# One written-out order of all engines exchanged for another in a one-core attention and MLP kernel

## The chip, the cores and the metric

The kernel runs on one core of one Trainium2 chip. The metric is the device time of one execution in microseconds (us); the figure of a kernel is the median of several executions. A core has five engines that take their instructions in order, each from its own queue: TensorE (PE; its weight loads are shown as PEld), VectorE (DVE), ScalarE (ACT), GpSimd (POOL) and SyncE (SP), which here only issues DMAs. Engines wait for one another, and for DMAs, by semaphores.

## What is computed

Windowed attention with four sink positions, over 4 batches, 8 heads, 768 positions and head size 64, and then an MLP over the 3072 tokens of width 512:

```
scores = q @ k.T / 8, kept where key < 4 or 0 <= query - key < 128
a      = softmax(scores);   x = (a @ v), heads side by side: 3072 x 512
h      = x @ w_in           (512 x 2048)
out    = (h * sigmoid(1.702 h)) @ w_out      (2048 x 512)
```

Inputs and output are float32 in memory; the kernel works in float16 and adds up in float32.

## The kernel before

The 3072 tokens are 24 blocks of 128 (block b is the part b mod 6 of batch b div 6). `BLOCKS` has the four that open a batch first (0, 6, 12, 18), then the others. A block needs its own keys and those of the block ahead of it (the window), and the four sink keys of its batch.

The work is a list of about 970 operations, each a closure that issues a few instructions on one engine. Their names, with the block or group number behind:

- `k`, `q`, `v`: loads of a block, with a cast to float16, issued by GpSimd (L310 for blocks 0, 6, 12, 18, 1 and 2, in long runs; L318 for the others; L271 for v). `wi`, `wo`: four pieces each of the two weights (L324, L331), also by GpSimd. All these share one DMA queue.
- `zv`: zeroing of `vsb` (L228), allowed on VectorE or GpSimd. `vsb`: its filling per batch (L344).
- `tk`, `tq`: transposes of k and q on TensorE (L383, L412) for the first eight blocks, with the copies `ck`, `cq` out of PSUM on VectorE or ScalarE (L241, L245). From block 5 on `tqk`, a DMA transpose issued by SP (L429), does this for one or two blocks.
- `msk`: the mask of blocks that open a batch (L464); `sc`: scores (L478, L483); `snk`: scores of the sinks (L507).
- `pk`, `mx`, `sb`, `ssb`, `ms`: masking, row maxima and subtraction on VectorE (L535 to L596); `nb` and `bx` instead for blocks that open a batch; `ex`: exponentials on ScalarE (L606).
- `ta`, `ca`: transposes of the weights on TensorE and their copies (L650), for the first six blocks; `tat`: the same as a DMA transpose by SP (L681) for the others. `sp`, `so`: GpSimd selects what belongs to the block ahead and to the own one (L637).
- `av`: values (L705 to L712); `nm`: their division (L722, L723); `tx`, `cx` or `txd`: the transpose to xT on TensorE (L740) or by DMA (L753).
- `h`: first layer (L786), `g`: its gate, on ScalarE (L816) or, with `th`, on ScalarE and VectorE (L800, L807) for groups 0 to 2; `o`: second layer (L836); `ev`: copy out; `st`: store (L856). Layers run in groups: {0}, {6}, {12, 18}, then two blocks each: group 3 is {1, 2}, group 4 {3, 4}, group 5 {5, 7}, and so on to group 12, {22, 23}.

PSUM tiles are rings: three of tag `mm` (all transposes and both layers), two of `sc`, one of `av`.

The order of everything is written out by hand, as the string `ORDER` (L56 on): a sequence of operation numbers, with a letter behind the number where an operation may go to several engines (d VectorE, a ScalarE, p GpSimd, s SP). `Plan.emit` (L125) calls the closures in this sequence. The costs, DMA classes and keys given to `plan.add` are kept in `Op` and read by nothing when the kernel is built:

```
for word in order.split():
    choice = letter.get(word[-1])
    op = self.ops[int(word[:-1] if choice else word)]
    assert all(d.seq in seen for d in op.deps), op.name
    seen.add(op.seq)
    op.emit(choice) if len(op.eng) > 1 else op.emit()
```

The first operations of the queues that matter here, decoded from the string, in the kernel before:

```
POOL  k0 q0 q6 q18 v0 k6 k12 wi1 k2 q12 k1 k18 vsb3 wi0 v6 wi2 q1 wi3 v12 wo0 wo1 v18 q2 wo2 wo3 q4 k4 k3 q3 k5 q7 q5
PE    msk0 tk0 tq0 tq6 sc0 tq18 tk6 tk12 ta0_0 ta0_1 msk6 av0_1 sc6 tk2 av0_0 tq12 tk1 tx0 tk18 h0_1 ...
      ... o6_3 sc2 tq4 snk2 ta1_1 tk4 o0_3 tx18 snk4 tq3 tk3 ta1_0 h2_7
SP    ... tat5 tqk9 tat7 st1_ st2_ tqk11 tat8 txd7 tat9 tqk13
```

Of the kernel before, what the change touches and what calls it, by code (L numbers as in the profile page):

```python
# [52 lines left out]


ORDER = """
3a 9 0s 7 14 94 4a 6 8d 5a 15 98 10 12 11 1a 13 18 2s 100 24 96 16 107 17 20 102 95d 88 103a 104 99d 29 105a 127 21  # L56
106 108 128a 26 173 109 23 112 174a 110 101p 97d 111 125 113 148 126d 86 114 115 149d 19 129 116a 117 130 90 118a 121
27 131 122 225 92 132 119 150 226a 120 22 194 151a 133 135 123 87 134 171 124d 136 152 89 613 137 172d 25 195d 138 614
153 175 139a 30 615 140 142 154 141a 143 610 155 158 144 91 616 611 145 612 146 617 156 93 147d 196 157 618 631 159
197d 160 628 36 632 161 176 35 162d 629 633 163 177 630 164a 637 181 178 32 167 619 638 182 168 183 179 622 639 180  # L60
165 634 166 33 620 623 635 38 621 198 636 199 640 204 42 200 227 201 641 228a 205 39 184 642 202 185a 188 206 186 624
189 187a 203 209 28 190 169 207 643 208 191 31 210 170d 229 644a 282 40 232 230 645 215 283a 280 231 625 216a 43 235
281a 233 192 217 626a 285 258 193d 256 34 627 259a 211 234 667 257a 41 236 212a 655 286 37 668 237 649 304 656 669 213
240 260 657 214 650 646 266 218 239 651 652 647 44 263 658 648 653 45 238 261 654 661 241 659 46 262 670 660 662 267
242 671 243a 264 221 663 244 664 265 245 672 268 665 222 246 284 666 247a 219 269 248 287 673 270 220 249 676 674a 288
271 48 252 290 677 49 253 675 223 323 291 47 250 224a 678 251 292 254 679 255a 289 272 293 688 680a 294 305 681 273
306 311 690 689 295 308 51 684 307 50 312 274 691 696 685 309 52 682 275 697 313 686 683 310 325 704 314 687 326 315
324 698 327 330 694 296 328 316 276 695 331 699 297 277 361 705 329 55 344 692 332 53 345 343 333 693 300 54 334 346
278 700 301 317 349 298 701 347 318 279a 335 299 706 702a 350 57 302 707 703 348 303a 58 351 321 708a 720 56 352 322
353 709 722 399 721 382 710 383 354 362 336 711 319 365 723 712 368 337 718 320 713 60 363 724 719 364 369 59 338 725  # L70
716 366 61 726 370 717 367 714 339 381 371 715 340 372 384 727 355 341 732 387 342 385 356 728 388 733 62 373 386 729
64 390 389 419 734 63 391 730d 359 744 360 392 752 745 374 400 731 357 403 735 375 753 358 742 406 736a 66 740 737 743
67 746 741 65 401 738 747 402 404 750 739 407 376 751 748 405 409 393 377 754 749 408 378 394 760 410 379 420 380 69
761 426 70 423 421 755 411 422 68 427 439 762 440 457 756 424 428 763 429 425 757 764a 430 766 765 758d 412 776 431
767 774 413 759 395 495 775 438 396 73 777 778 444 71 441 768 779 445 72 397 769 772 442 398 788 773 446 416 443 770
417 432 780 447 771 448 789 433 414 75 782 415 74 790 781 418 783 76 434 449 791 435 458 792a 459 464 784 793 461 800
460 465 806 514 801 462 796 807 466 477 798 797 467 478 450 463 436 799 785 437 468 451 794 786d 497 79 787 476 498
804 482 795 77 469 479 452 78 802 483 805 480 816 803 484 810 485 453 808 481 470 454 486 496 455 811 499 471 456 502
516 817 500 81 809 812 487 503 82 818 501 80 504 813 505 517 506 819 814d 474 815 820d 832 475 821 488 824 833 507 472
489 834 473 552 825 515 84 835 535 518 828 83 521 836 829 536 85 522 490 837 822 519 826 523 823 508 491 844 827 520  # L80
509 492 524 534 525 493 830 537 494 540 838 538 831 845 526 541 839 539 590 573 542 846 574 543 553 544 840 559 556
847 527 841 848a 545 862 528 842a 849 510 863 864 843 511 856 865 554 850 555 857 546 560 512 851 858 513 547 557 854
859 561 529 855 852 558 530 860 853 562 563 866 531 872 532 572 861 533 873 575 578 548 564 867 576 549 874 579 868
577 875 581 580 869 582 876d 591 565 877 870d 550 594 871 888 566 551 583 882 597 889 592 884 593 595 569 883 878 570
885 596 886 879 598 880 887 584 599 567 881 600 890 568 601 585 900 571 894 901 891 602 588 902 589 892 895 893 910
603 903 911 914 904a 604 586 905 915 920 587 906 921 912 907 605 913 918 606 916 919 607 917 908 608 896 609 909 922
897 928 898a 923 899 929 924 930 940 931 941 944 932a 925 933 945 948 926a 936 927 949 938 937 942 939 934 943 946 935
956 947 950 957 951 958 952 962 953 963 954a 959 964 955 960a 965 961 966a 967
"""


# [64 lines left out]
def kernel(  # L156
# [207 lines left out]
    for pos, b in enumerate(BLOCKS):  # L364
# [9 lines left out]
        if b in OCT:  # L374
            parts = []
            before = used_slot.pop(SLOT[b], [])
            for w in (1, 0):
                tp = ps("mm", (P, 8, 4, 16), FP32, f"t{'qk'[w]}{b}")

                def t_qk(w=w, buf=buf, n=n, tp=tp):  # L380
                    for t in range(8):
                        for l in range(2):
                            nc.tensor.matmul(  # L383
                                tp()[64 * l : 64 * l + 64, t], buf()[:, n, w, t],
                                ident.rearrange("p (j l u) -> p l j u", l=2, u=16)[:, l], start=True, stop=True,
                            )
# [15 lines left out]
            o_qkt[b] = parts  # L402
        elif b in TQ:
            tp = ps("mm", (P, 8, P), FP16, f"tq{b}")
            parts = []
            before = used_slot.pop(SLOT[b], [])
            for w in (1, 0):

                def t_qk(w=w, buf=buf, n=n, tp=tp):
                    src = buf()[:, n, w].rearrange("p h d -> p (h d)")  # L410
                    for c in range(4):
                        nc.tensor.transpose(tp()[:, 4 * w + c], src[:, bass.ts(c, P)], ident)  # L412
# [12 lines left out]
            o_qkt[b] = parts  # L425
        elif n == 0:

            def t_qk(buf=buf, unit=unit, s=SLOT[b]):
                nc.sync.dma_start_transpose(  # L429
                    qkT[:, s : s + len(unit)].rearrange("p r c t -> p (r c) t"),  # L430
                    buf()[:, 0 : len(unit)].rearrange("p n w h d -> p (n w h d)"),
                )
# [26 lines left out]
        if r == 0:  # L459

            def mask(sc=sc, own=own):
# [437 lines left out]
```

## Time and profile before

| | |
|---|---|
| median of 3 runs | 235.01 us (234.93 to 235.21) |
| profiled execution | 236.26 us, span of its instructions 234.6 us |
| TensorE busy | 220.5 us |
| VectorE busy | 153.1 us |
| ScalarE busy | 145.9 us |
| GpSimd busy | 111.5 us |
| DMA | 32.07 MB |

The span runs from the first instruction to the last of one profiled execution; that execution's own time includes what lies around the span. Busy time is the union of an engine's instructions; a matmul's end is modelled. An idle stretch is put down to the event that came last before it ended. Line numbers are those of the kernel file; the copies out of PSUM all stand on the lines of the helper `copy` (L241, L245).

### The profile page before, as it was taken

Reading aid. Unit: us, or ns where it says so; the run is one execution under the profiler, and the core shown is the slowest. Engines: PE = TensorE matmul, PEld = TensorE weight load, DVE = VectorE, ACT = ScalarE, POOL = GpSimd, SP = SyncE. Lnnn points to the kernel's source line nnn. Section 1 sums busy time; section 2 is a strip of 40 time slices with the busy share of each in tenths; the row PEclk is TensorE's granted clock in tenths of the full one; section 3 lists DMA queues with packets and bytes.
Section 4 is the critical chain, followed back from the end, with each engine's and each line's share of the span. In section 5 each row is a group of like instructions: output and inputs, shape, how many; then the busy total and the mean of one; then the engine's idle time right before and its main releaser. Section 6 shows DMA issues by size and latency. Waiting matters only on the chain.

```text
span 234.6 us, 5452 instructions
## 1 busy us (share of the span) xinstructions
PE 220.5 (94%) x2202; PEld 151.6 (65%) x2202; DVE 153.1 (65%) x384; ACT 145.9 (62%) x226; POOL 111.5 (48%) x129
## 2 busy tenths in 40 slices
PE   0899999999999998898999999999999999999994
PEld 0669865776575685476487577586496595775763
DVE  4668889999789959838846498969755982120000
ACT  2556866975586884464385576887678477541632
POOL 8964545966367829449178082656240330300000
PEclk9999999999999999999999999999999999999999
DMA  5999999999999999999999999999951445121202
GB/s 82 177 197 199 199 197 171 186 160 70 171 210 140 130 202 145 113 232 120 135 258 126 189 134 127 102 267 100 137 140 21 109 110 95 48 39 50 90 2 89
DMA packets 120904, 32.07 MB, mean 137 GB/s; under 512 B 112016, under 2 KB 117936, under 8 KB 120880
## 3 DMA queue, kind: packets, MB, share of 16 engines
q0 software_dynamic: 69888, 13.64, 72.7%
q1 hardware_dynamic: 50512, 17.96, 40.3%
q8 instruction: 17, 0.28, 0.5%
q10 hardware_dynamic: 480, 0.13, 0.3%
q14 instruction: 7, 0.06, 0.1%
HBM read 27.46 MB, written 6.29 MB: 144 GB/s over the span
## 4 chain that ended last, share of the span: by engine, by line
PE 70%; DVE 18%; DMA 6%; POOL 3%; issue 1%; ACT 0%; POOLq 0%
PE o L836 28%; PE hT L786 28%; DVE mx L545 4%; DMA qkn<-in_q_dram 4%; PE sc L483 4%; DVE sc L535 3%; DVE mx L548 3%; DVE e L582 3%; DMA xT<-xn 2%; PE av L705 2%; PE av L710 2%; POOL qkn L310 2%; DVE gT L807 2%; DVE xn L723 2%; PE av L712 2%; DVE e L596 1%
## 5 line engine op out<-in xcount | busy, mean ns | idle before, releaser
L786 PE MATMUL hT<-xT,w_in 128*128 128x256 f16 (+1 forms) x832 | 94.1, 266 | 1.0 <-DMA xT<-xn 1.0
L836 PE MATMUL o<-w_out,gT 128*128 128x512 f16 (+2 forms) x400 | 91.5, 371 | 0.1
L786 PEld LDWEIGHTS <-w_in 128*128 128x128 f16 x832 | 74.2, 98 | 13.2 <-issue 2.7
L816 ACT ACTIVATE gT<-hT 128x512 f16<-128x512 f32 x80 | 46.2, 597 | 31.1 <-PE hT L786 30.9
L836 PEld LDWEIGHTS <-gT 128*128 128x128 f16 x400 | 36.3, 98 | 33.4 <-issue 1.1
L637 POOL TENSOR_SCALAR_AFFINE_SELECT atp<-at 128x1024 f16<-128x1024 f16 (+1 forms) x22 | 22.4, 1018 | 74.0 <-DMA at<-a 67.4
L545 DVE TENSOR_REDUCE mx<-sc 128x4 f32<-128x512 f32 x48 | 32.5, 682 | 0.6 <-PE sc L478 0.6
L535 DVE COPY_PREDICATED sc<-later,sc 128x512 f32<-128x512 uint16 x40 | 26.5, 690 | 8.9 <-PE sc L483 8.7
L582 DVE TENSOR_TENSOR e<-sc,mx 128x512 f32<-128x512 f32 x40 | 26.4, 682 | 0.0
L722 DVE RECIPROCAL rcp<-av 128x4 f32<-128x4 f32 x48 | 8.5, 177 | 27.2 <-PE av L712 25.1
L606 ACT ACTIVATE a<-e 128x1056 f16<-128x1056 f32 (+2 forms) x24 | 22.4, 935 | 4.1 <-issue 2.3
L271 POOL DMA_DIRECT2D v<-in_v_dram x24 | 21.5, 896 | 3.8 <-DMA w_out<-in_moe_w_out_dram 1.7
L637 POOL TENSOR_SCALAR_AFFINE_SELECT at<-at 128x1024 f16<-128x1024 f16 (+1 forms) x22 | 22.1, 1008 | 1.4
L606 ACT ACT_TABLE_LOAD x13 | 16.7, 1283 | 9.7 <-issue 5.8
L723 DVE TENSOR_TENSOR xn<-av,rcp 128x256 f16<-128x256 f32 x48 | 20.4, 424 | 1.7
L816 ACT ACT_TABLE_LOAD x14 | 18.0, 1283 | 3.5 <-PE hT L786 3.3
L710 PE MATMUL av<-v,at 128*128 128x65 f16 x192 | 17.6, 196 | 0.9 <-POOL at L637 0.9
L318 POOL DMA_DIRECT2D qkn<-in_q_dram x18 | 16.1, 894 | 3.8 <-DMA w_out<-in_moe_w_out_dram 2.6
L318 POOL DMA_DIRECT2D qkn<-in_k_dram x18 | 16.1, 892 | 2.6 <-DMA w_out<-in_moe_w_out_dram 1.5
L710 PEld LDWEIGHTS <-at 128*128 128x128 f16 x192 | 14.4, 99 | 4.4 <-POOL at L637 1.2
L245 ACT COPY osb<-o 128x512 f32<-128x512 f32 (+2 forms) x14 | 7.7, 555 | 13.3 <-PE o L836 9.6
L712 PE MATMUL av<-v,atp 128*128 128x65 f16 x160 | 15.1, 194 | 0.0
(57 smaller groups left out, 199.8 us busy)
## 6 DMA issues: line engine op xcount, KB each, us to landing
out_dram<-osb SPq DMA_DIRECT2D x23, 256.0 KB, 3.1
qkn<-in_k_dram POOLq DMA_DIRECT2D x24, 128.0 KB, 5.9
qkn<-in_q_dram POOLq DMA_DIRECT2D x24, 128.0 KB, 5.9
v<-in_v_dram POOLq DMA_DIRECT2D x24, 128.0 KB, 6.4
w_in<-in_moe_w_in_dram POOLq DMA_DIRECT2D x4, 512.0 KB, 10.2
w_out<-in_moe_w_out_dram POOLq DMA_DIRECT2D x4, 512.0 KB, 13.4
at<-a SPq DMA_TRANSPOSE x18, 3.3
qkT<-qkn SPq DMA_TRANSPOSE x10, 7.7
```

The source lines that it names most:

```text
L271: f"v{b}", POOL, 0.88, lambda b=b, view=view: nc.gpsimd.dma_start(v65[:, b, :, 0:D], view),
L318: lambda buf=buf, n=n, w=w, view=view: nc.gpsimd.dma_start(buf()[:, n, "qk".index(w)], view),
L535: nc.vector.copy_predicated(out=t()[:, :, :, own].rearrange("p l j s -> p (l j) s"), mask=later.unsqueeze(1).to_broadcast((P, 4, P)), data ...
L545: nc.vector.tensor_reduce(out=part, in_=t()[:, :, :, own], axis=AX.X, op=ALU.max)
L582: nc.vector.tensor_tensor(out=e32()[:, 512 * hf : 512 * hf + 512].rearrange("p (l j s) -> p l j s", l=2, j=2), in0=t()[:, :, :, own], in1= ...
L606: nc.scalar.activation(out=a16()[:, lo:hi], in_=e32()[:, lo:hi], func=AF.Exp, scale=scale)
L637: nc.gpsimd.affine_select(out=dst, in_=at()[:, lo : lo + num], pattern=[[0, num], [1 if own else -1, P]], compare_op=ALU.is_ge if own else ...
L710: nc.tensor.matmul(av()[:, i], at()[:, c], v65[:, b, h], start=(r == 0), stop=(r == 0))
L723: nc.vector.tensor_tensor(out=xn()[:, xi, 4 * hf : 4 * hf + 4].rearrange("p (j l) d -> p l j d", l=2), in0=av()[:, :, 0:D].rearrange("p (l ...
L786: nc.tensor.matmul(ht()[:, n].rearrange("p (n t) -> p n t", n=NT), w_in16[:, c, bass.ts(f, P)], t0()[:, i0 : i0 + NT, c], start=(c == 0), ...
L816: lambda fs=fs, gt=gt, ht=ht: nc.scalar.activation(out=gt()[:, fs[0] : fs[-1] + 1], in_=ht(), func=AF.Gelu_apprx_sigmoid),
L836: nc.tensor.matmul(po()[:, 0:width], gt()[:, F, bass.ts(t, P)], w_out16[:, F, c0 : c0 + width], start=(F == 0), stop=(F == NF - 1),)
```

## The change

The string `ORDER` is replaced as a whole; the operations are the same ones. Three planner costs are changed as well: they enter no instruction.

```diff
 ORDER = """
-3a 9 0s 7 14 94 4a 6 8d 5a 15 98 10 12 11 1a 13 18 2s 100 24 96 16 107 17 20 102 95d 88 103a 104 99d 29 105a 127 21
...
+1a 9 4s 10 11 8p 100 12 2a 7 6 13 0a 94 5a 98 3a 15 96 14 23 107 17 21 101d 26 104 95d 105a 20 102 99d 29 103a 171 97d
...
-                    f"t{'qk'[w]}{b}", PE, 0.45 if early else 0.376, t_qk, deps=[ld["qk"[w], b], o_ident],
+                    f"t{'qk'[w]}{b}", PE, 0.4 if early else 0.376, t_qk, deps=[ld["qk"[w], b], o_ident],
...
-                    f"t{'qk'[w]}{b}", PE, 0.44 if early else 0.226, t_qk, deps=[ld["qk"[w], b], o_ident],
+                    f"t{'qk'[w]}{b}", PE, 0.25 if early else 0.226, t_qk, deps=[ld["qk"[w], b], o_ident],
...
-                f"msk{b}", PE, 0.88 if early else 0.45, mask, deps=[o_bias0, o_identb], take=sc, key=K0 - 34
+                f"msk{b}", PE, 0.6 if early else 0.45, mask, deps=[o_bias0, o_identb], take=sc, key=K0 - 34
```

Decoded, the same queues in the changed kernel:

```
POOL  zv q0 k0 k18 k6 q12 k1 k12 k2 q6 v0 v6 q1 q18 wi1 wi3 wi2 wi0 wo0 v12 wo1 v18 q2 wo2 wo3 k3 q4 k4 q3 v1 v3 q5 k5
PE    msk0 tq0 tk0 tk18 sc0 tk6 tq12 tk1 tk12 tk2 tq6 ta0_0 msk6 ta0_1 av0_0 sc6 tq1 av0_1 tq18 tx0 snk1 ta6_0 h0_1 ...
      ... o6_3 sc2 tx18 ta1_0 o0_3 tk4 tq4 tk3 tq3 h2_2
SP    ... tat5 tqk9 tat7 st1_ tqk11 st2_ tat8 txd7 tat9 tqk13
```

These change their engine: `zv` from VectorE to GpSimd, where the built program has it as a memset of 128 x 2080 elements (128 x 1040 words of 32 bits on VectorE); `vsb3` from GpSimd to VectorE; the copies ck6, ck18, ck1, cq1, ca12_0, cx12, cx18, ev8, ev15 from VectorE to ScalarE; cq6, ck2, ca6_0, ca12_1, ca18_0, ca1_1, ck4, ev18, ev9 from ScalarE to VectorE; and three constant loads between SP and ScalarE. On every engine the sequence differs over most of its length.

More of the change, by code (lines that the diff above doesn't have):

```diff
@@ L55 @@
 ORDER = """
-3a 9 0s 7 14 94 4a 6 8d 5a 15 98 10 12 11 1a 13 18 2s 100 24 96 16 107 17 20 102 95d 88 103a 104 99d 29 105a 127 21
[L57 to L85, printed above, removed]
@@ L86 @@
-603 903 911 914 904a 604 586 905 915 920 587 906 921 912 907 605 913 918 606 916 919 607 917 908 608 896 609 909 922
-897 928 898a 923 899 929 924 930 940 931 941 944 932a 925 933 945 948 926a 936 927 949 938 937 942 939 934 943 946 935
-956 947 950 957 951 958 952 962 953 963 954a 959 964 955 960a 965 961 966a 967
+1a 9 4s 10 11 8p 100 12 2a 7 6 13 0a 94 5a 98 3a 15 96 14 23 107 17 21 101d 26 104 95d 105a 20 102 99d 29 103a 171 97d
+108 18 172a 125 106 16 109 150 126a 112 19 194 151a 110 195a 113 148 27 111 149d 225 24 226d 127 114 88 115 152 128d
@@ new lines @@
+92 116a 130 129 90 117 119 131 118a 120 86 196 132 121 173 87 197a 122 174a 22 133 135 123 134 199 175 89 124d 138 136
+200 25 137 613 139d 30 142 614 153 143 140 615 154 141a 91 619 155 158 144 620 156 145 157 159 621 146 93 616 147d 160
+637 617 634 638 618 32 176 639 635 631 636 177 632 610 178 36 633 161 611 179 35 181 628 162a 612 180 163 182 165 622
+164d 166 183 184 33 167 623 185d 629 168 28 198 630 188 204 34 169 640 201 170a 205 227 641 228a 189 39 186 206 624
+187a 202 209 230 642 231 203 215 190 38 207 643 208 216d 191 210 217 229 644a 43 192 235 645 211 193a 625 232 31 212a
@@ new lines @@
+236 280 37 282 626a 256 233 258 283a 627 652 41 259a 281d 234 257a 649 213 653 238 237 40 261 241 661 650 654 214 239
+262 260 651 42 662 285 242 263 304 240 655 218 243a 286 663 44 219 656 646 266 45 657 658 647 220 244 664 648 659 46
+267 670 665 245 660 221 671 264 222 246 672 247a 269 265 248 250 268 667 249 666 270 284 251 49 676 668 271 290 47 669
+252 677 287 48 253 323 673 288 254 674a 678 291 255a 675 289 306 223 679 292 224a 293 682 307 272 294 680d 305 683 681
+688 273 311 295 308 684 50 312 689 686 51 685 309 692 52 313 687 310 276 693 690 314 277 315 704 344 324 345 705 330
@@ new lines @@
+691 316 327 325 694 326 331 274 695 296 696 275 361 328 698 697 297 332 278 699 279a 329 53 298 333 334 343 54 299 700
+346 317 349 300 701 347 55 335 706 301 702a 318 350 302 703 707 303a 348 57 716 351 399 708a 58 352 362 353 56 709 319
+365 717 712 354 368 336 720 320 713 321 337 722 721 322 714 59 723 363 61 718 715 364 366 60 340 719 710 369 724 367
+711 371 370 726 725 341 372 732 338 733 355 339 381 342 382 356 384 727 387 734 64 373 383 388 728 63 385 419 735 62
+389 359 736a 390 729 386 737 360 391 750 374 730d 742 392 751 375 752 731 401 67 400 743 402 738 753 406 65 403 378 66
@@ new lines @@
+739 746 407 379 748 747 404 376 749 740 408 377 744 741 405 357 409 745 420 358 410 754 393 423 380 426 439 760 440
+394 421 755 411 422 68 424 761 427 70 457 756 425 69 762 429 428 757 430 412 766 758d 431 438 413 767 772 444 759 441
+72 397 763 445 773 73 442 768 764a 71 398 770 765 769 443 495 416 446 771 788 447 417 448 780 414 458 415 432 774 461
+781 449 464 459 433 789 460 462 395 775 74 778 396 75 776 465 418 779 76 463 436 777 782 466 437 790 467 468 783 791
+450 784 792d 469 451 434 785 435 78 793 802 786a 514 79 800 803 77 454 798 787 455 470 801 476 799 794 482 471 479 452
@@ new lines @@
+795 808 453 80 796 456 809 81 477 806 797 478 82 480 804 807 483 474 805 816 481 475 810 484 497 817 485 498 486 496
+516 502 818 499 811 487 503 822 500 552 812 504 823 501 819 505 517 813 820d 506 488 472 821 814d 824 473 489 815 836
+825 507 535 83 515 536 828 518 85 837 521 492 84 829 834 519 493 826 835 522 490 827 508 830 520 491 832 831 509 523
+494 844 524 833 525 534 845 590 537 540 838 538 526 846 541 839 539 542 864 543 544 840 512 865 545 527 553 513 847
+556 528 559 573 841 848a 574 849 510 842a 852 511 843 546 860 853 529 861 547 850 530 854 851 554 866 855 555 557 531
@@ new lines @@
+856 532 560 858 533 857 558 867 859 562 561 550 872 563 551 862 592 868 593 863 564 591 873 597 594 548 880 598 595
+869 881 599 565 888 870a 600 596 874 871 889 566 549 601 886 875 567 876d 572 887 602 568 882 575 569 877 578 883 884
+570 892 579 571 885 576 878 893 603 580 890 879 581 577 604 894 891 582 900 895 912 583 901 913 607 902 608 896 910
+584 897 911 916 585 898a 605 899 917 914 606 918 915 908 919 586 909 906 587 903 907 588 904a 922 589 905 920 609 923
+921 928 924 929 925 930 926a 948 927 931 949 938 932a 940 933 939 936 941 946 937 934 947 942 935 950 943 956 944 957
@@ L89 @@
+945 951 958 952 962 953 963 954a 959 964 955 960a 965 961 966a 967
 """
```

## Prediction, made before the changed kernel ran

> **What bounds the kernel now.** I read the page first, then busy time by stage, then TensorE's waits.
>
> ```profile
> span 234.6 us, 5452 instructions
> PE 220.5 (94%) x2202; PEld 151.6 (65%) x2202; DVE 153.1 (65%) x384; ACT 145.9 (62%) x226; POOL 111.5 (48%) x129
> ```
>
> TensorE (PE) is busy 94% of the span, so only 234.6 - 220.5 = 14.1 us are there to be won or to grow. The profiled execution took 236.26 us around this span; the median of the runs is 235.01. Sums below are made on the span and added to the median, since an idle microsecond of the span is one of the run. About 0.2% (0.47 us) is what a measurement of this kernel can tell from no change.
>
> Busy time by stage; the columns after the stretch are its length, then busy time (and instructions) of PE, PEld, DVE, ACT, POOL:
>
> ```profile
> 0.00:20.00 20.00, 12.87 (x221) 9.68 (x222) 12.03 (x34) 9.83 (x25) 15.46 (x26) 1.00 1.14 157
> 20.00:44.00 24.00, 23.27 (x316) 16.82 (x314) 20.76 (x54) 16.37 (x39) 13.71 (x17) 1.00 1.66 188
> 44.00:62.40 18.40, 18.30 (x173) 12.30 (x171) 17.90 (x43) 11.44 (x22) 11.79 (x16) 1.00 1.81 135
> 62.40:231.60 169.20, 166.03 (x1501) 112.83 (x1499) 102.39 (x257) 107.93 (x140) 70.56 (x72) 1.00 1.00 127
> ```
>
> PE idles 20.00 - 12.87 = 7.13 us in the first 20 us, 0.73 in the next 24, 0.10 from 44.00 to 62.40 (where VectorE is busy 17.90 of 18.40, 97%), and 3.17 from there to its end at 231.6; the last 3 us of the span are the last output leaving. A row of PE hides what a slow start costs, because a pipelined matmul counts as busy while it drains; so for the start I go by when a named piece of work begins. For the rest I go by waits, of PE in the stretch 62.4 to 231.6 (us in total, times, longest):
>
> ```profile
> PE hT L786 <- DMA xT<-xn: 1.0, 1, 1.0
> PE av L710 <- POOL at L637: 0.9, 1, 0.9
> PE av L705 <- DVE xn L723: 0.6, 1, 0.6
> ```
>
> These three are 2.5 of the 3.17 us. The change adds and drops no matmul, so the new time is the start, plus the same PE work, plus whatever waits the new order has.
>
> **The change part by part.** The three edited costs emit nothing; cost 0. What counts is the order, and in it these steps.
>
> *Step 1: the zeroing of vsb (`zv`, L228) goes from VectorE to the head of GpSimd's queue, ahead of every load.*
>
> ```profile
> 0.92 0.28 DVE L229 MEMSET vsa<- 32x260 f32 x1 [0.92 <-PEq L880]
> 1.32 0.78 POOL L310 DMA_DIRECT2D qkn<-in_k_dram  x1 [0.81 <-POOLq L880]
> 2.26 0.93 DVE L228 MEMSET vsb<- 128x1040 uint32 x1 [0.16 <-issue]
> 9.12 1.26 POOL L344 TENSOR_TENSOR vsb<-vsa,ownm 32x520 f16<-32x520 f32 x1
> 10.40 0.68 DVE L344 TENSOR_TENSOR vsb<-vsa,ownm 32x520 f16<-32x520 f32 x1
> L637 POOL TENSOR_SCALAR_AFFINE_SELECT atp<-at 128x1024 f16<-128x1024 f16 (+1 forms) x22 | 22.4, 1018 | 74.0 <-DMA at<-a 67.4 <-ACT at L245 4.1 <-PE snk L507 2.5
> ```
>
> The trace has no such memset on GpSimd. Below: VectorE's 0.93 us. Above: GpSimd's select makes 1024 elements in 1.018 us, 0.99 ns each, and the new program's memset has 2080 f16 elements, so 2.07 us. Between: L344 takes 1.26 on GpSimd against 0.68 on VectorE, 1.85 times, which makes 1.72 of 0.93. I take 1.8. The first VectorE instruction starts at 0.92, so GpSimd can start the memset then too; the first load is issued at 0.92 + 1.8 = 2.7 instead of 1.32: **1.4 us later**. Ends: 0.92 + 0.93 - 1.32 = 0.5, and, if the memset starts only at 1.32, 2.07.
>
> The Trainium skill (GPSIMD Engine Reference, 4.1 Engine selection) speaks against this move in general, elementwise work being VectorE's, but has one-input operations at roughly line rate there; its section 3.1 gives 1.03 cycles an element, which at its 1.2 GHz would be, as an estimate, 1.79 us here and 1.4 us for the delay. The nearest row, the select, is a little slower than that; no row of the trace shows the memset itself.
>
> What waits behind it? All loads, in one queue. When do they come?
>
> ```profile
> L310 POOL DMA_DIRECT2D qkn<-in_k_dram x1: 780/780/780, 1.3 to 1.3; - x1
> DMA to landing us min/median/max: 4.2/4.2/4.2
> ```
>
> ```profile
> POOL qkn L318 <- DMA w_out<-in_moe_w_out_dram: 4.1, 3, 1.8
> ```
>
> ```profile
> L318 POOL DMA_DIRECT2D qkn<-in_q_dram x1: 873/873/873, 32.1 to 32.1; - x1
> ...
> DMA to landing us min/median/max: 10.5/10.5/10.5
> ```
>
> The first rows are the first load (issued 1.32, landed 5.5), the last ones that of q of block 3, the 28th load (issued 32.14, landed 42.7). Landing grows from 4.2 to 10.5 us although GpSimd waits for room in the queue in between (three waits of 4.1 us at L318 alone): from 5.5 on the queue is never empty, and it sets the pace, not the issue. The same 27 loads stand ahead of `q3` in the new order, all eight weight pieces among them. So `q3` lands at 42.7 + 1.4 = 44.1 in any order of them. Its user:
>
> ```profile
> 43.20 0.61 PE L412 MATMUL tq<-ident,qkn 128*128 128x128 f16 x8
> 43.72 0.44 PE L650 MATMUL ta<-ident,a 128*128 128x128 f16 x5
> 44.00 1.24 PE L786 MATMUL hT<-xT,w_in 128*128 128x256 f16 x9
> ```
>
> Before, `tq3` (first of the x8) starts at 43.20, 0.5 after the landing; then `tk3` and `ta1_0`, and group 2's first layer at 44.00. In the new order `tq3` comes last, right ahead of group 2, and `ta1_0` earlier. Four transposes take about 0.25 (half of 43.72 - 43.20), so group 2 starts at 44.1 + 0.25 = 44.35, **+0.35 us**. In general it is the delay less 1.05: with 0.5 it is nothing, PE's own work then being the limit, and with 2.07 it is +1.0. What comes earlier in the new order (transposes ahead of weights) cannot win more than this gate lets through. Since the queue is the limit, `vsb3` leaving GpSimd (1.26 us) wins nothing there.
>
> *Step 2: evacuations change engines.* VectorE gives away zv (0.93) and nine copies, takes vsb3 (0.68) and nine copies, of these lengths:
>
> ```profile
> L241 DVE COPY osb<-o 128x512 f32<-128x512 f32 x7 | 4.8, 692 | 1.4 <-PE o L836 1.3
> L241 DVE COPY xT<-tx 128x512 f16<-128x512 f16 x4 | 1.7, 420 | 1.1 <-PE tx L740 1.1
> ```
>
> Over the whole kernel that is nothing. In the stretch from 44.0 to 62.4, where it has half a microsecond to spare, it gains `ck4` and loses `cx18` (0.42 each); `ev18_` (0.69) goes on it just ahead of block 5. The second-layer and `sc` steps there wait for VectorE's g and sb pieces, and in the new order `g2_6` and `g2_7` stand behind more of block 3's and 4's work. I take **+0.2**, with -0.5 (nothing but the better place of block 2's chain) to +0.9 (both `ev18_` and a g piece in the way) as ends.
>
> *Step 3: waits of the steady stretch.* PE work between two instructions is counted from the new order with these pieces:
>
> ```profile
> 83.34 0.89 PE hT L786 x8
> 84.23 0.54 PE sc L483 x8
> 93.83 5.66 DMA xT<-xn
> ...
> 102.44 0.86 PE o L836 x4
> ```
>
> ```profile
> 92.44 0.28 PE L705 MATMUL av<-vsb,at 128*128 128x260 f16 x1
> ...
> 92.81 5.34 PE L836 MATMUL o<-w_out,gT 128*128 128x512 f16 x24
> ```
>
> (values of half a block: 92.81 - 92.44 = 0.37.)
>
> Between the last values of blocks 5 and 7 and the first layer of their group stood 6 o and 1 av; now 1 sc and 1 snk more, about 0.6 us: of the 1.0 us wait for xT (landing 5.66 us after issue) **-0.6**. From the scores of block 7 to its values the work is the same (8 h, 7 o, 5 av, 2 sc, 2 tx), so that 0.9 us wait stays. But other distances shrink: block 11 had 12 h, 10 o, 5 av between scores and values, now 9, 8 and 4, some 5 us less; blocks 10, 17, 19, 20 and 21 lose 2.5 to 3.6 us. The shortest distance that ran without a wait before is block 22's 7 h, 9 o, 4 av, 1 sc: 6.2 + 7.7 + 1.5 + 0.5 = 15.9 us. In the new order blocks 19, 20, 23 (and 7) stand at 16.0 to 16.5, just over it. Their transposes must then land as fast as the fast ones do. I take **+0.6** for one or two short waits, with 0 and 2.5 as ends. Two table loads fewer on ScalarE (26 for 28 in the programs) lie beside PE, none of whose long waits names ScalarE: 0.
>
> Sum: 0.35 + 0.2 - 0.6 + 0.6 = +0.55; 235.01 + 0.55 = **235.6 us**.
>
> **The rivals.**
> (B) *Faster, because the transposes stop being late.* The costliest waits, 1.0 and 0.9, end on transposes:
>
> ```profile
> at<-a SPq DMA_TRANSPOSE x18, 3.3
> ...
> xT<-xn SPq DMA_TRANSPOSE x8, 4.3
> ```
>
> ```profile
> L681 SPq DMA_TRANSPOSE at<-a x1: 1617/1617/1617, 78.8 to 78.8; - x1
> ...
> DMA to landing us min/median/max: 7.7/7.7/7.7
> ```
>
> ```profile
> 73.49 1.81 SPq L429 DMA_TRANSPOSE qkT<-qkn  x1
> ```
>
> Block 7's (issued 78.8) took 7.7 us against the page's median of 3.3, and xT's 5.66 against 4.3; block 9's 16-slice transpose was issued 5.3 us ahead of block 7's on the same queue. If the new order issues them into a shorter backlog, both waits go (-1.9), with +0.35 at the start: 233.5. Against it: on SP block 9's is still issued right ahead of block 7's. It decides when block 7's lands in under 7.7 - 0.9 = 6.8 us.
> (C) *No difference*: step 1 is hidden (memset near 0.93) and waits come and go alike; 235.0.
> (D) *Clearly slower*: the shorter distances of step 3 are caught by late transposes (7.7 in place of 3.3 us), in three to five blocks at 0.5 to 0.9 each, 2.5 in place of my 0.6: 235.6 + 1.9 = 237.5. For it: blocks 19 to 23 have little over the shortest distance. Against it is the page's DMA row, a digit for 5.9 us:
>
> ```profile
> DMA  5999999999999999999999999999951445121202
> ```
>
> From the 31st digit (176 us) on there is hardly a backlog, and most of their transposes fall there.
> That the change doesn't act is not possible: all engines' orders differ.
>
> **How the numbers follow.** Forecast 235.6 (range of its own 235.0 to 236.5) 0.34; B 0.28; C 0.24; D 0.14. The bound for faster is 234.54, for slower 235.48. B is faster; C and a little of the forecast are the same; the rest is slower: faster 0.28, same 0.28, slower 0.44. The range takes in B and D: 233.4 to 237.5.
>
> **What would show it.** Step 1: a GpSimd memset of 1.7 to 2.1 us from 0.9, first load issued at 2.7 and group 2's first layer at 44.2 to 44.6. Step 2: VectorE busy over 95% from 44 to 62, and the next group's first layer at 62.6 to 63.2. Step 3: the xT wait at group 5 down to about 0.4, the 0.9 of block 7 still there, and new short waits at values of blocks 19 to 23. I am wrong if group 2 starts before 44.0 (the queue wasn't the limit), or if PE idles after 62.4 under 2 or over 5 us.

## The result, and the profile after

The changed kernel is **faster**: 234.41 us median of 22 runs against 235.23 us of 22 runs of the kernel before beside them, ratio 0.9942 (95% interval 0.9919 to 0.9965), about 1.4 us less. The forecast was 235.6, no faster. Ratios are of undisturbed runs, those within 1.5% of the kernel's fastest (the two medians of all 22 would give 0.9965), and the profiles of `before_2` and `after_no_max`, which are of disturbed ones, are left out of the readings below.

The profiled execution of after took 235.79 us, among its longer ones. Its page, first lines and the DMA row:

```profile
span 234.1 us, 5451 instructions
...
PE 217.5 (93%) x2202; PEld 151.3 (65%) x2202; DVE 150.2 (64%) x384; ACT 143.6 (61%) x224; POOL 111.7 (48%) x129
...
DMA  3999999999999999999999999999632343313202
```

PE is busy 3.0 us less with the same 2202 matmuls, while the span is only 0.5 shorter. With the same matmuls, whose ends are modelled, that is no work saved, and most of it lies at the start, as busy time by stage of after shows (columns as before):

```profile
0.00:20.00 20.00, 11.42 (x229) 8.58 (x229) 11.74 (x36) 10.05 (x23) 16.79 (x26) 1.00 1.06 140
20.00:44.00 24.00, 21.97 (x291) 15.86 (x292) 19.29 (x50) 15.73 (x41) 11.13 (x14) 1.00 1.59 191
44.00:62.40 18.40, 18.18 (x188) 12.71 (x186) 17.96 (x44) 11.10 (x21) 13.44 (x18) 1.00 2.01 150
62.40:231.60 169.20, 165.90 (x1501) 114.14 (x1498) 101.23 (x258) 106.73 (x140) 70.39 (x72) 1.00 0.98 128
```

Up to 44 us PE is busy 33.39 of after's time against 36.14 of before's. Step 1's rows in after's timeline, then the load of q3, then its users on PE:

```profile
0.80 1.83 POOL L228 MEMSET vsb<- 128x2080 f16 x1 [0.29 <-POOLq L880]
2.58 0.78 POOL L310 DMA_DIRECT2D qkn<-in_q_dram  x1
```

```profile
L318 POOL DMA_DIRECT2D qkn<-in_q_dram x1: 873/873/873, 34.5 to 34.5; - x1
...
DMA to landing us min/median/max: 10.0/10.0/10.0
```

```profile
43.69 1.20 PE L412 MATMUL tq<-ident,qkn 128*128 128x128 f16 x16
44.72 0.49 PE L786 MATMUL hT<-xT,w_in 128*128 128x256 f16 x3
```

The memset took 1.83 us (forecast 1.8), the first load goes out 1.26 later, q3 lands at 34.5 + 10.0 = 44.4, and group 2 starts at 44.72 instead of 44.00. So after pays at the start and must win later. PE's waits in 62.4 to 231.6 don't show it:

```profile
PE av L710 <- POOL at L637: 1.9, 2, 1.2
PE hT L786 <- DMA xT<-xn: 0.9, 1, 0.9
```

2.8 us against the 2.5 of before. One profile each isn't enough here, so I cut all profiles at four places where both orders have done the same matmuls (form by form, counted along PE's queue in the trace: 728, 862, 1186 and 1638 of the 2202). Length of each stage in us, from the start of one of these matmuls to the next; the kernels are those of the experiments:

```
order and kernel            to 728  to 862 to 1186 to 1638  to end | PE ends
old  before                  64.57   13.58   37.64   48.54   67.23 |  231.57
     before_snk_apart        63.70   14.88   36.27   50.70   67.02 |  232.56
     before_zv_pool          65.06   13.64   34.81   50.53   67.01 |  231.05
mix  head_after (new, old)   64.99   13.11   36.43   49.68   67.01 |  231.22
     tail_after (old, new)   64.53   13.47   37.14   48.13   67.02 |  230.29
new  after                   65.21   13.12   36.80   48.87   67.05 |  231.05
     after_2                 64.58   13.12   37.16   48.80   67.03 |  230.69
     after_snk_apart         64.32   13.12   37.75   48.84   67.03 |  231.07
     after_zv_vector         63.42   13.12   35.89   49.32   67.02 |  228.78
small VectorE steps that can't be blocked:
old  before_no_lock          63.55   14.30   34.63   49.80   67.01 |  229.29
     before_no_max           63.87   13.94   34.88   49.58   67.01 |  229.28
     before_zv_pool_no_lock  64.09   13.75   34.88   49.45   68.19 |  230.37
mix  tail_after_no_lock      63.32   13.94   35.41   48.13   66.87 |  227.67
new  after_no_lock           64.95   13.11   35.71   47.73   66.86 |  228.37
     after_zv_vector_no_lock 63.56   13.11   36.38   47.95   66.86 |  227.87
     after_zv_vector_no_max  62.76   13.11   36.57   47.82   66.85 |  227.12
```

(In the mixes the first two stages have the one order, the rest the other; "PE ends" is the end of TensorE's last matmul.) Means in the upper part, by the order that a stage has: to 728, old with zv on VectorE 64.27 (three), new with it on GpSimd 64.78 (four), **+0.5**; to 862, 13.89 (four) and 13.12 (five), **-0.8**; to 1186, 36.29 and 36.95, **+0.7**; to 1638, 49.86 and 48.79, **-1.1**; to the end, 67.07 and 67.03. The sum is -0.7 us, a little under the timed gain of 0.8 to 1.9; each row is one execution. The third stage's lengths overlap between the orders (34.8 to 37.6 and 35.9 to 37.8); in the second every new one is shorter than every old one, in the fourth too but for before's 48.54. The gain is thus made in two places, and paid for at the start. It is a matter of TensorE's waits: a stage's length less the waits of over 0.1 us in it is 13.1 to 13.5 us in the second stage, 34.6 to 35.2 in the third and 47.7 to 48.4 in the fourth, in all sixteen profiles.

### The profile page after: what moved, and what is told of

Its sections match the earlier page's. It is cut to its first block, busy times and chain, and to the rows that moved or that the text cites. A ratio compares the mean times of both kernels' runs of the same rounds, so it can differ in the third digit from the quotient of the medians.

```text
span 234.1 us, 5451 instructions
## 1 busy us (share of the span) xinstructions
PE 217.5 (93%) x2202; PEld 151.3 (65%) x2202; DVE 150.2 (64%) x384; ACT 143.6 (61%) x224; POOL 111.7 (48%) x129
## 3 DMA queue, kind: packets, MB, share of 16 engines
q1 hardware_dynamic: 50272, 17.96, 39.7%
## 4 chain that ended last, share of the span: by engine, by line
PE 67%; DMA 22%; DVE 5%; POOL 4%; issue 1%; ACT 1%; SPq 0%; POOLq 0%
PE o L836 29%; PE hT L786 27%; DMA w_out<-in_moe_w_out_dram 7%; DMA at<-a 6%; PE sc L483 3%; DMA xT<-xn 3%; DMA v<-in_v_dram 3%; DMA qkn<-in_k_dram 2%; PE av L710 2%; PE av L712 2%; PE av L705 1%; DVE sc L535 1%; POOL at L637 1%; POOL atp L637 1%; DVE mx L545 1%; POOL vsb L228 1%
## 5 line engine op out<-in xcount | busy, mean ns | idle before, releaser
L836 PE MATMUL o<-w_out,gT 128*128 128x512 f16 (+2 forms) x400 | 92.6, 371 | 0.7 <-DMA w_out<-in_moe_w_out_dram 0.7
L786 PEld LDWEIGHTS <-w_in 128*128 128x128 f16 x832 | 73.8, 98 | 15.9 <-issue 3.7
L637 POOL TENSOR_SCALAR_AFFINE_SELECT atp<-at 128x1024 f16<-128x1024 f16 (+1 forms) x22 | 22.4, 1017 | 74.6 <-DMA at<-a 61.2
L836 PEld LDWEIGHTS <-gT 128*128 128x128 f16 x400 | 35.8, 97 | 33.2 <-issue 2.2
L535 DVE COPY_PREDICATED sc<-later,sc 128x512 f32<-128x512 uint16 x40 | 26.0, 691 | 7.4 <-PE sc L483 7.1
L606 ACT ACTIVATE a<-e 128x1056 f16<-128x1056 f32 (+2 forms) x24 | 22.3, 935 | 8.7 <-issue 5.8
L637 POOL TENSOR_SCALAR_AFFINE_SELECT at<-at 128x1024 f16<-128x1024 f16 (+1 forms) x22 | 22.4, 1017 | 1.2
L723 DVE TENSOR_TENSOR xn<-av,rcp 128x256 f16<-128x256 f32 x48 | 20.4, 425 | 1.7
L245 ACT COPY osb<-o 128x512 f32<-128x512 f32 (+2 forms) x15 | 8.4, 557 | 16.7 <-PE o L836 16.6
```

The lines of the kernel that those rows point to most:

```text
L535: nc.vector.copy_predicated(out=t()[:, :, :, own].rearrange("p l j s -> p (l j) s"), mask=later.unsqueeze(1).to_broadcast((P, 4, P)), data ...
L606: nc.scalar.activation(out=a16()[:, lo:hi], in_=e32()[:, lo:hi], func=AF.Exp, scale=scale)
L637: nc.gpsimd.affine_select(out=dst, in_=at()[:, lo : lo + num], pattern=[[0, num], [1 if own else -1, P]], compare_op=ALU.is_ge if own else ...
L723: nc.vector.tensor_tensor(out=xn()[:, xi, 4 * hf : 4 * hf + 4].rearrange("p (j l) d -> p l j d", l=2), in0=av()[:, :, 0:D].rearrange("p (l ...
L786: nc.tensor.matmul(ht()[:, n].rearrange("p (n t) -> p n t", n=NT), w_in16[:, c, bass.ts(f, P)], t0()[:, i0 : i0 + NT, c], start=(c == 0), ...
L836: nc.tensor.matmul(po()[:, 0:width], gt()[:, F, bass.ts(t, P)], w_out16[:, F, c0 : c0 + width], start=(F == 0), stop=(F == NF - 1),)
```

## The experiments

**The new order once more, its two halves, and `zv` put back.** Behind the 403rd operation both strings have done the same ones: head_after has the new string up to there and the old one behind it, tail_after the reverse. after_zv_vector has this edit in the new order:

```diff
-1a 9 4s 10 11 8p 100 12 2a 7 6 13 0a 94 ...
+1a 9 4s 10 11 100 12 2a 7 6 8d 13 0a 94 ...
```

> The changed kernel once more, beside the two spliced orders. Theory T (the gain is made in the steady stretch, from about 65 us on): ratio to before 0.992 to 0.997 as in the first timing, and group 2's first layer again later than before's 44.0 us. Theory S (the gain is made at the start): the same ratio. It gives a second profile: in the first one the changed kernel took 235.79 us, over its median of 234.41, so its waits were perhaps not those of a usual execution; PE's waits for transposes and for GpSimd (2.7 us there) are then under 1.5 us here.

> The first 403 operations (to the scores of block 8, some 78 us) in the new order, all others in the old order; the set of the 403 is the same in both orders. Theory T: the start costs about 0.7 us (group 2 began at 44.72 for 44.00, group 3 at 63.14 for 62.40) and nothing is won behind it: ratio 1.002 to 1.004. Theory S: the whole gain is here: 0.994, 233.6 to 234.0 us where before has 235.2.

> The first 403 operations in the old order, all others in the new order. Theory T: the whole gain without the cost of the start: ratio 0.988 to 0.992, some 2 us under before. Theory S: nothing, 0.999 to 1.001.

> The new order with the zeroing of vsb back on VectorE (after the zeroing of ksb), so that the first load is issued at about 1.3 us instead of 2.6. Theory that the load queue paces the start: every load lands 1.2 us sooner, group 2's first layer starts 0.5 to 0.8 us sooner than with the new order, and the time falls by 0.5 to 0.8 us (ratio to before 0.989 to 0.992). Rival, that the later issue is hidden because the queue catches up or other waits take its place: within 0.2 us of the new order.

Measured, each against before timed beside it: after_2 0.9946 (0.9907 to 0.9985), the result again. head_after 1.0001 (0.9966 to 1.0035), tail_after 0.9977 (0.9943 to 1.0011): neither half alone is told from no change by its time, and the table says why the head is worth nothing: +0.7 to matmul 728 and -0.8 behind it. Theory T, which gave the tail 0.988 to 0.992, missed too. after_zv_vector 0.9886 (0.9844 to 0.9929), 233.94 us: clearly faster than before, with nothing left out, and 0.6% under after_2, though the two intervals overlap. Its rows:

```profile
1.32 0.77 POOL L310 DMA_DIRECT2D qkn<-in_q_dram  x1 [0.81 <-POOLq L880]
...
2.48 0.93 DVE L228 MEMSET vsb<- 128x1040 uint32 x1 [0.16 <-issue]
```

```profile
42.30 1.06 PE L412 MATMUL tq<-ident,qkn 128*128 128x128 f16 x16
43.19 2.00 PE L786 MATMUL hT<-xT,w_in 128*128 128x256 f16 x14
```

The first load is back at 1.32 and group 2 starts at 43.19, 0.8 ahead of before and 1.5 ahead of after. In the table's profiles the first load decides this, whatever the order behind it: group 2 starts at 42.83 to 44.00 (mean 43.50) in the nine with that load at 1.32, and at 44.09 to 45.02 (mean 44.45) in the seven with it at 2.58. Whether the new order is the better one at the start they don't show, as before_snk_apart, an old one, has group 2 at 43.13.

**The memset in the old order, and the sinks apart.** before_zv_pool moves `zv` alone (it, before_2 and the tail_after kernels also have the three new planner costs, which enter no instruction). The snk_apart kernels test another theory of mine, that PE waits because sink scores and values share the one PSUM place `av`: the sinks get two places of their own in that bank (columns 320 and 384 on, in turn, the values keeping 0 to 259). The first two lines are before_zv_pool's edit, the others that of the snk_apart kernels.

```diff
-3a 9 0s 7 14 94 4a 6 8d 5a ...
+8p 3a 9 0s 7 14 94 4a 6 5a ...
...
+    avbank = psp.tile([P, 512], FP32, tag="av", bufs=1, name="avbank")
...
-            snk = ps("av", (P, 4, 2, 4), FP32, f"snk{b}")
+            snk = Buf("av", snk_make)
...
-            av = ps(AVR.get((b, hf), "av"), (P, 4, D1), FP32, f"av{b}_{hf}")
+            av = Buf("av", av_make)
```

> The old order with one thing moved: the zeroing of vsb at the head of GpSimd's queue. The step that the prediction priced at 0.35 us. Theory that the load queue's start carries through to the end: the queue's landings come 1.3 to 2.2 us later, group 2's first layer at 44.8 to 45.8 instead of 44.0, time +0.8 to +1.8 us, ratio 1.003 to 1.008. Rival, that half a microsecond of margin and later waits take most of it (the prediction's price): +0.2 to +0.4 us, ratio 1.001 to 1.002.

> The old order, with the sink scores written to two places of their own in the one PSUM bank that they share with the values, so that sink scores and values no longer wait for VectorE to empty one another's tile. Theory that the new order's gain in the steady stretch is the smaller waits for this hand-over (sinks of block 8, values of blocks 9, 13 and 16 in the old order's profile, 1 us in idle and about as much in pieces too short to be called idle): 1.0 to 2.0 us less than before, ratio 0.992 to 0.996, and TensorE's waits for VectorE's ss and xn gone. Rival, that the gain lies in the waits for transposes: within 0.3 us of before.

> The new order with the same two places for the sink scores. Hand-over theory: little is left to win here, 0 to 0.5 us less than the new order (ratio to before 0.991 to 0.995), and old and new order stand closer together than without the places. Rival (transposes): the same as the new order, 0.994.

> The kernel before, unchanged, timed as if it were another: the ratio shows what the timing can tell apart, 1.000 with an interval of about 0.004 to both sides. Its profile is a second one of the old order: the theory of the steady stretch has TensorE's waits for VectorE's ss and xn in it again, and 168.5 to 169.5 us from group 3's first layer to the end of TensorE's work (167.9 and 168.2 in the two profiles of the new order); if it has 168 or less, the stretch's gain was a chance of one profile.

before_zv_pool 1.0013 (0.9983 to 1.0043), to matmul 728 65.06 against 64.27, +0.8: the time can't be told from no change, though in its profile the start is 0.8 later. before_snk_apart 1.0000 (0.9967 to 1.0032) and after_snk_apart 0.9940 (0.9906 to 0.9974): each like its own order, so the theory of the shared place **fell**. before_2, the old kernel against itself, 0.9993 (0.9967 to 1.0018), shows what the method tells apart. Yet one of these profiles shows a wait that can come in the second stage. before_snk_apart's timeline (its lines stand 10 lower: L606 is L596, L647 L637, L715 L705, L733 L723):

```profile
75.30 1.76 DVE L606 TENSOR_TENSOR e<-ss,mx 128x32 f32<-128x32 f32 x1
...
75.53 0.28 PE L715 MATMUL avbank<-vsb,at 128*128 128x260 f16 x1
75.88 1.12 POOL L647 TENSOR_SCALAR_AFFINE_SELECT atp<-at 128x1024 f16<-128x1024 f16 x1
...
77.78 0.42 DVE L733 TENSOR_TENSOR xn<-avbank,rcp 128x256 f16<-128x256 f32 x1
...
78.26 0.27 PE L715 MATMUL avbank<-vsb,at 128*128 128x260 f16 x1 [1.12 <-DVE xn L733]
```

A subtraction of 32 columns, 0.18 us elsewhere, takes 1.76 us. It begins while GpSimd issues a load (75.00 to 75.90) and ends at 77.06, just behind GpSimd's select (77.00). The division of the half of block 4 that is done first waits behind it on VectorE, and the other half's values, with one value place and only four matmuls of `o` and the transposes tx3 between the halves, wait for the division. The new order has eight matmuls of scores and four of `o` there. The same place in after_2's timeline, without a wait:

```profile
75.30 0.18 DVE L596 TENSOR_TENSOR e<-ss,mx 128x32 f32<-128x32 f32 x1
75.50 0.27 PE L705 MATMUL av<-vsb,at 128*128 128x260 f16 x1
...
76.27 0.42 DVE L723 TENSOR_TENSOR xn<-av,rcp 128x256 f16<-128x256 f32 x1
...
77.37 0.27 PE L705 MATMUL av<-vsb,at 128*128 128x260 f16 x1
```

That is one profile. In before this place costs 0.2 us, in before_zv_pool and tail_after nothing. The second stage's other waits are at the sinks of block 8, for a division on VectorE (before 0.2, before_zv_pool 0.5), and for a select (tail_after 0.3, before_snk_apart 0.3).

**Small steps that GpSimd can't block.** Is the new order better because these stalls fall elsewhere? Groups of VectorE in before, and the durations of one line (min/median/max in ns):

```profile
L548 DVE TENSOR_TENSOR mx<-mx,ms 128x4 f32<-128x4 f32 x40 | 10.8, 271 | 1.4
L596 DVE TENSOR_TENSOR e<-ss,mx 128x32 f32<-128x32 f32 x20 | 6.8, 341 | 0.0
```

```profile
L548 DVE TENSOR_TENSOR mx<-mx,ms x40: 161/164/994, 36.6 to 192.4; 128x4 f32<-128x4 f32 x40
```

The mean of L548 is 271 where the median is 164: a few long ones. The 60 steps of these two lines take 15.0 to 19.8 us in the four profiles with the old order behind the 403rd operation, and 13.6 to 15.9 in the five with the new one. The no_lock kernels put one-input reductions of the same sizes in their place (row maxima don't take in the sinks, and the sinks' scores aren't reduced by the maximum); the no_max kernels drop L548 alone, the second diff, which leaves the result as it is: a softmax doesn't depend on the number subtracted.

```diff
-                    nc.vector.tensor_tensor(out=part, in0=part, in1=ms[:, 4 * hf : 4 * hf + 4], op=ALU.max)
+                    nc.vector.tensor_reduce(
+                        out=spare[:, 4 * hf : 4 * hf + 4], in_=ms[:, 4 * hf : 4 * hf + 4].unsqueeze(2), axis=AX.X, op=ALU.max
+                    )
...
-                nc.vector.tensor_tensor(
+                nc.vector.tensor_reduce(
...
-                    in0=ss().rearrange("p (h s) -> p h s", s=4),
-                    in1=small.unsqueeze(2).to_broadcast((P, 8, 4)),
-                    op=ALU.subtract,
+                    in_=ss().rearrange("p (h s) -> p h s", s=4).unsqueeze(3), axis=AX.X, op=ALU.max,
```

```diff
-                if ms is not None:
-                    part = small[:, 4 * hf : 4 * hf + 4]
-                    nc.vector.tensor_tensor(out=part, in0=part, in1=ms[:, 4 * hf : 4 * hf + 4], op=ALU.max)
```

> The old order; the 60 small VectorE steps that read two tensors in SBUF (the maximum of mx and ms, the subtraction from the sink scores) are replaced by reductions of the same sizes that read one. Left out is so the part of the sinks in the maximum, which the softmax doesn't need, and the subtraction of the maximum from the sink scores, which it does. Blocking theory (these steps stand still while GpSimd selects, 5 to 10 us in all over their 10 us unblocked in five profiles of the old order, 3.6 to 5.9 in five of the new one, and that is the new order's gain): VectorE's busy time falls by 5 to 10 us, the time by 1.5 to 3 us, ratio 0.988 to 0.994. Rival, that the blocked time is slack on VectorE and the gain comes from the order itself: within 0.5 us of before, ratio 0.998 to 1.000.

> The same replacement in the new order (the same parts left out). Blocking theory: less to win than in the old order, 0.7 to 1.5 us from the new order, and old and new order without blocking are equal within 0.5 us or the new one is the slower by its start: ratio 0.989 to 0.993. Rival: the new order keeps its whole lead of 0.5 to 0.6% over the old one, both treated alike.

> The same replacement in the new order with the zeroing of vsb on VectorE (the same parts left out). Queue theory: 0.8 to 1.4 us less than the new order with the replacement alone, as the first load starts 1.26 us sooner. Rival, that the 0.6% of the first such run was the blocking's chance: within 0.3 us of it.

> The same replacement in the old order with the zeroing of vsb at the head of GpSimd's queue (the same parts left out). If the price of the later load queue is the same in both orders, 0.8 to 1.4 us over the old order with the replacement alone. If the old order has the margin that the prediction saw, 0.2 to 0.5 us.

> The first 403 operations in the old order, the others in the new one, with the 60 VectorE steps replaced as before (the sinks' part of the maximum and the subtraction from the sink scores left out). Blocking theory (the new order's lead in the steady stretch is blocking avoided): the same as the old order so treated, ratio to before 0.985 to 0.989. Transposes theory (the lead is waits for DMA transposes avoided): the lead stays, 1.5 to 2 us under the old order so treated, 0.978 to 0.981.

> The old order without the 40 maximum steps of L548 (left out: the sinks' part of the subtracted maximum, from which the result doesn't depend). Blocking theory: most of the 3 us that replacing all 60 gave, 2 to 3 us less than before, ratio 0.988 to 0.992; the 6 us of VectorE's own work saved give little more, since VectorE is busy 65%.

> The new order without the same 40 steps (the same part left out). Blocking theory: equal to the old order without them within 0.5 us. Transposes theory: 1.3 us under it, as with the steps.

> The new order with the zeroing of vsb on VectorE and without the same 40 steps (the same part left out). Both theories: the fastest that gives the whole result, 1.3 to 2.5 us under the new order without the steps, 231 to 232 us, ratio 0.979 to 0.983.

| | as it is | no_lock | no_max |
|---|---|---|---|
| before | 1 | 0.9867 (0.9816 to 0.9918) | 0.9865 (0.9818 to 0.9912) |
| after | 0.9942 (0.9919 to 0.9965) | 0.9876 (0.9815 to 0.9936) | 0.9890 (0.9839 to 0.9941) |
| after_zv_vector | 0.9886 (0.9844 to 0.9929) | 0.9783 (0.9722 to 0.9843) | 0.9886 (0.9846 to 0.9925) |
| before_zv_pool | 1.0013 (0.9983 to 1.0043) | 0.9891 (0.9828 to 0.9953) | |
| tail_after | 0.9977 (0.9943 to 1.0011) | 0.9819 (0.9774 to 0.9863) | |

The reductions of before_no_lock, one line lower:

```profile
L549 DVE TENSOR_REDUCE spare<-ms 128x4 f32<-128x4 f32 x40 | 5.9, 147 | 0.0
L599 DVE TENSOR_REDUCE e<-ss 128x32 f32<-128x32 f32 x20 | 3.5, 176 | 0.0
```

The stalls cost the old order 1.3% (0.8 to 1.8), 3 us. None of the profiles without them in the table has a PE wait for VectorE behind 62.4 us. By the times alone the new order's lead is gone without them (0.9876 against 0.9867, 0.9890 against 0.9865, each within about 0.6%), as the theory of the stalls has it. With `zv` on VectorE in both orders the times disagree: 0.9783 against 0.9867, a lead of 0.8%, but 0.9886 against 0.9865, none. For the 0.9886 both theories had 0.979 to 0.983 and missed. The table of stages speaks **against** it as the whole cause: without stalls the new order is still shorter in the second stage (13.11; 13.75 to 14.30) and in the fourth (47.73 to 48.13; 49.45 to 49.80). What it gives back is the third stage (35.41 to 36.57; 34.63 to 34.88) and, by `zv` on GpSimd, the start (64.95; 63.55 and 63.87; with `zv` on VectorE 63.56 and 62.76). And tail_after_no_lock's 0.9819 is below before_no_lock's, as far as the intervals tell. In the place of the stalls come late transposes; before_no_lock's waits of PE in 62.4 to 231.6:

```profile
PE hT L787 <- DMA xT<-xn: 1.6, 1, 1.6
PE snk L508 <- DMA qkT<-qkn: 1.1, 1, 1.1
```

The first is group 7 in the fourth stage, the second block 7's sinks in the second. All three old kernels without stalls wait at group 7 (1.6, 1.3, 1.4 us), and before_zv_pool's waits behind 62.4, stalls and all, are

```profile
PE hT L786 <- DMA xT<-xn: 2.4, 1, 2.4
PE snk L507 <- DVE xn L723: 0.5, 1, 0.5
```

with group 7 the first of them. That is four of the seven profiles with the old order there. Of the nine with the new one only after waits there (0.9, its wait for xT above). Between the last values of blocks 10 and 11 and group 7's first layer the old order has 20 matmuls of `o`, 8 of `sc`, one `av` and one `snk`, the new one 16 of `h`, 24 of `o` and two `av`; by the prediction's rows (0.89 for 8 h, 0.86 for 4 o, 0.54 for 8 sc, 0.37 for av; a snk 0.24, as at 68.76 in before) 5.5 and 7.7 us, 2.2 more. So I take the gain to be in **distances**, whichever of two late things, a stalled VectorE or a transpose, happens to be last at that place. This is argued: no run changes one distance alone.

## Why the prediction was wrong, point by point

- *Step 1, +0.35, and step 2, +0.2: right in sum, by luck.* The mechanism is as forecast (1.83 us of memset, first load at 2.58, q3 at 44.4, group 2 at 44.72; 44.24 in after_2). To matmul 728, which lies behind 62.4, the new order costs +0.5 for the 0.55 of the two steps. But between the orders group 2 moves by 0.65 (44.35, the mean of after, after_2 and after_snk_apart, against 43.70, that of before, before_snk_apart and tail_after): the margin of 1.05 that step 1 took off the delay was at most half of that, as `zv` alone, in before_zv_pool, moves group 2 by 0.8 us (44.49 against 43.70) for a load 1.26 later. And step 2's +0.2 didn't come: from group 2's first layer to group 3's it is 18.40 us in before and 18.42, 18.27 and 18.16 in the three new ones. VectorE is busy 17.96 of 18.40, over 95% as forecast.
- *"What comes earlier in the new order cannot win more than this gate lets through"* leaves out what the gate itself costs. With the first load at 1.32 the new order starts group 2 at 43.19; zv costs it 1.3 us to matmul 728 (64.70, the mean of after, after_2 and after_snk_apart, less 63.42), and 0.6% by the times (0.9946 and 0.9886), not 0.35. In the second pair it is 0.9% (0.9876 and 0.9783), in the third nothing (0.9890 and 0.9886), with about 0.6 either way. In the old order zv costs 0.8 us to matmul 728, and 0.5 without the stalls (64.09 less 63.55).
- *Step 3 is the one that failed.* "So that 0.9 us wait stays" and the -0.6 at group 5 came true in the main: the wait at block 7's select is 0.67 in after and 0.91 in tail_after, though in none of the other three new profiles, and group 5 waits for no transpose there nor in after_2, tail_after and after_zv_vector (1.07 in after_snk_apart). But the **+0.6 at blocks 19, 20 and 23 never came**: behind matmul 1638 both orders take 67.0 us, and no wait ends there in the upper nine profiles. That alone makes +0.55 into nothing. A wait of just this kind came at a place that step 3 doesn't name, block 9, whose distance from scores to values shrinks by 8 matmuls of `h`, 0.9 us. In after the transpose took 7.3 us to land, and the values waited for the select behind it:

```profile
102.56 1.09 POOL L637 TENSOR_SCALAR_AFFINE_SELECT atp<-at 128x1024 f16<-128x1024 f16 x1 [6.35 <-DMA at<-a]
...
104.87 0.20 PE L710 MATMUL av<-v,at 128*128 128x65 f16 x1 [1.19 <-POOL at L637]
```

Eight of the nine profiles with the new order there wait for this select (0.6 to 1.8 us), none with the old one. What outweighs it are waits of the old order that step 3 put at nothing, since before's one profile hardly shows them: in the second stage block 8's sinks, the selects and block 4's halves (-0.8), in the fourth group 7 (2.37 in before_zv_pool) and block 11's values behind block 10's division (1.03 in head_after, 0.89 in before_snk_apart) (-1.1). Behind matmul 728 step 3 had 0.0, and the stages have -1.2; the timed -1.4 for the whole against the stages' -0.7 stays unexplained. I counted the places of which before's profile showed a wait (group 5, block 7) or which shrank by much.
- *What step 3 took for the kernel's waits was one execution's.* Of the three rows (1.0, 0.9, 0.6) the first and the third come back in head_after (0.9, 0.5) and before_snk_apart (0.9, 0.4) in the same stage, none in before_zv_pool, whose 2.4 at group 7 no other of these has.
- *Rival B* (faster, transposes no longer late) named the right sign, and its 233.5 lies 0.9 off where the forecast is 1.2 off. Its places were wrong: block 7's wait stays in after and tail_after, and at block 9 a late transpose adds one, the larger part of the third stage's +0.7. *C* failed, as the waits of the second and fourth stages don't come and go alike. *D* was wrong as the reason given against it has it: in no profile of the new order does a wait end behind matmul 1638 (164 us).
- *The signs to watch for* were too weak: group 2 not before 44.0 and PE idle 2.75 us after 62.4 both lie in what I had called right. One profile's idle time doesn't show the gain: in the second to fourth stages TensorE waits 2.9 to 5.0 us in the three old profiles and 2.2 to 3.5 in the four new ones.

What stays open: how the lead divides between stalls and transposes. The times say that most of it goes with the stalls, the stages that the two gains don't, and both within 0.6%. Nor was any of the copies that change their engine moved by itself.

## What to carry to other kernels

Price a reordering at every short distance that it changes, not only at the waits of one profile: a wait hides the next one, and where executions differ by half a per cent another profile shows another list. Cut the traces where both orders have done the same work, and compare stage by stage; time the two halves and the single moved operations. Look at min, median and max of the small instructions: a mean far over the median is a stall with a cause. And put nothing at the head of a queue that is full from then on: here 1.26 us there came back as 1.3 in the new order, by matmul 728, and as 0.8 in the old one.

## What the runs showed of the hardware

A VectorE operation with two inputs in SBUF stands still while GpSimd's select runs. In before's timeline:

```profile
87.80 1.09 POOL L637 TENSOR_SCALAR_AFFINE_SELECT at<-at 128x1024 f16<-128x1024 f16 x1
88.14 0.75 DVE L548 TENSOR_TENSOR mx<-mx,ms 128x4 f32<-128x4 f32 x1
...
89.53 0.16 DVE L548 TENSOR_TENSOR mx<-mx,ms 128x4 f32<-128x4 f32 x1
```

Four columns take 0.16 us, or 0.75 and an end together with the select's (88.89). Of the 60 such steps of before 15 take over 0.23 us, and 13 of them end within 0.1 us behind a select; the other two (0.68 and 0.99 us) lie beside GpSimd's issuing of loads. Four unstretched ones overlap a select: three start with it or just ahead of it, one in its last 0.12 us. Over 40 and 20 such steps of before that is 10.8 + 6.8 us in place of 40 x 0.16 + 20 x 0.18 = 10.0. One-input reductions of the same size took 147 and 176 ns on average, and none of them over 0.18 us, though 11 ran beside a select (before_no_lock). The Trainium skill (SBUF — State Buffer, Who interferes with whom) states this: two SBUF inputs contend with a GpSimd instruction that reads SBUF, the ports that they share are an exclusive lock, and a reduction never contends. The trace agrees for the selects, and adds the price: 1.3% of this kernel, through 60 instructions that need 10 us in all.
